# RetNet block and SwiGLU feed-forward on one core: the row norm of units 3 to 8 by block turns on VectorE and a 16-column product

## The chip, the cores and the metric

The kernel runs on one core of a Trainium2 chip. The metric is the device time of one execution in microseconds (us); the figure of a version is the median over its runs. The three runs of the kernel before took 1104.19, 1106.02 and 1107.22 us, so its median is 1106.02 us.

## The reference

Eight batches of eight heads, sequence 576, head size 64, go through a causal retention without softmax. The result is laid out as 4608 rows of 512 numbers and goes through an RMS norm and a SwiGLU feed-forward of inner width 1536. All of it is float32.

```python
scores = scale * np.matmul(q, k.transpose(0, 1, 3, 2))
gamma = 1.0 - 2.0 ** (-5.0 - np.arange(H, dtype=np.float32))
Dmat = np.where(rel >= 0, gamma[:, None, None] ** rel[None, :, :], 0.0)
x = np.matmul(scores * Dmat[None, :, :, :], v)            # -> (B*S, H*D)
rms = np.sqrt(np.mean(x * x, axis=-1, keepdims=True) + 1e-06)
xn = x / rms * rms_g
g = xn @ w_gate
out = (g * (1.0 / (1.0 + np.exp(-g))) * (xn @ w_val)) @ w_out
```

The part that matters here is `rms`: for each of the 4608 rows one sum of 512 squares, and the inverse root of it, with which the whole row is multiplied.

## The kernel before, in words

The 4608 rows are worked off in nine **units** of 512 rows, numbered 0 to 8. A unit's `x` lies turned in SBUF: the 512 features in four chunks of 128 partitions, the 512 rows along the free dimension (`x_of[u]`, 128 x 4 x 512). The sum over a row's features is therefore a sum over four chunks and 128 partitions.

Units 0 and 1 and the rounding of the weights are woven together by a written-out plan (`PLAN`, in `start`). From unit 2 on, one loop (lines 1283 to 1316) does for each unit u: six calls of `up(u, n)`, each 7 block products of a Strassen-like scheme (gate and value projections, into `h`); between them, up to four attention slots that make the `x` of later units; then `across(u)`, seven products of the output projection, again in blocks. Everything is issued in program order under a manual schedule, so the order on each engine is the order of the calls. `up` and `across` are generators that yield after each block product, and the loop puts the small steps of the next unit's norm behind chosen yields.

The norm of the next unit, u+1, stands as follows in this order:

- behind the first four products of `up(u, 5)`: `square` (line 458, ScalarE) squares chunk i, and `gather` (467, 473, VectorE) adds it to the running sum. After four chunks `t_of[u+1]` is one tile of 128 x 512 whose column sums are the sums of squares.
- behind the fifth product (i == 4): `root_1`. One matmul (504) multiplies the 128 x 512 tile with a 128 x 128 tile of ones, which leaves the column sums, the same in all 128 partitions, in a PSUM bank `ms`. Then an inverse square root by a guess from the bits and a polynomial step each, on full 128 x 512 tiles: ScalarE at 506, VectorE's `y` and `e` at 510 and 513, ScalarE's squares at 509 and 516, VectorE at 517.
- in `across(u)` behind the second yield after the first (i == 2): `root_2` (526, 529, VectorE, 128 x 512 tiles), which leaves the inverse root in an SBUF tile.
- i == 3 to 6: `scale_x` (548, VectorE), one chunk each: `x = x * rms_k * root`.
- i == 8: `sums_of_x` (563, VectorE): the block sums that the next unit's `up` multiplies.

All PSUM tiles come from one pool of eight banks. `up` takes four banks each call (`x`, `y`, `z`, `w`), `across` takes eight (`xo`, `xp` and so on, in the order of their products x, z, x, z, y, w, x), and `ms` one. `inner_sums` (766, 771, GpSimd) makes block sums that `across` multiplies; `second_operand` (775) and `last_operand` (779) are VectorE's share of the same. Units 0 and 1 have a norm of their own (`norm_1`, line 481: 16 products with one moving column each), and unit 2's `root_1` and `root_2` are called from the plan.

Of the kernel before, what the change touches and what calls it, by code (L numbers as in the profile page):

```python
# [10 lines left out]
F32 = mybir.dt.float32  # L11
U32 = mybir.dt.uint32
AF = mybir.ActivationFunctionType
ALU = mybir.AluOpType
P = 128
L = P // 2
SQ = 32
# [27 lines left out]
def kernel(  # L45
# [11 lines left out]
    nc = tc.nc  # L57
    B, H, S, D = q.shape
    NTOK, DM = out.shape
# [6 lines left out]
    U = 512  # L66
# [8 lines left out]
    K0, K1 = 2.38924456, 0.703952253  # L75
# [4 lines left out]
    const = ctx.enter_context(tc.tile_pool(name="const", bufs=1))  # L80
# [3 lines left out]
    tmp = ctx.enter_context(tc.tile_pool(name="tmp", bufs=4))  # L84
# [4 lines left out]
    def bank(name):  # L89
        return banks.tile([P, 512], F32, tag="b", name=name)  # L90
# [4 lines left out]
    def row(name):  # L95
        return tmp.tile([P, U], F32, tag="n", name=name, bufs=3)

    def cell(name, value):
        t = const.tile([P, 1], F32, name=name)
        nc.vector.memset(t, value)  # L100
        return t

    ones = const.tile([P, P], F32, name="ones")
    ident = const.tile([P, P], F32, name="ident")
# [3 lines left out]
    most = cell("most", 1151.0 + 7.5 / 16)  # L108
    top = cell("top", 255.0 * 2.0**23)
    guess = cell("guess", 0x5F1FFFF9 + 2.0**22 * np.log2(DM))  # L110
    causal = const.tile([P, L], F32, name="causal")
    gq = const.tile([P, NHP, L], F32, name="gq")
    gp = const.tile([P, NHP, 2], F32, name="gp")
# [36 lines left out]
    x_of, t_of = {}, {}  # L150
# [103 lines left out]
    def prepare(j):  # L254

        d = st[j]
        for odd in range(2):
            t = d["qraw"][:, odd::2]
            nc.scalar.activation(
                out=t, in_=t, func=AF.Copy, scale=gp[:, jobs[j][1], odd : odd + 1]  # L260
            )
        for nm in ("q", "k"):
            t = att.tile([P, S], F32, tag=nm + "T", name=f"{nm}T_{j}")
            nc.vector.transpose(out=t, in_=d.pop(nm + "raw").rearrange("p t a -> p (t a)"))
            d[nm + "T"] = t
        scale_v(j)
# [105 lines left out]
    def values(j):  # L372

        d = st[j]
        av = d["av"] = [bank(f"av_{j}_{i}") for i in range(2)]
        for c in range(NC):
            i, odd = divmod(c, 2)
            for e in range(2):
                mm = nc.tensor.matmul(  # L379
                    av[odd][column(j, odd, e), i * L : i * L + L],  # L380
                    lhsT=d["v"][side(odd), i, e] if c < NC - 1 else d["vt"][:, e],
                    rhs=d["ret"][side(odd), e, i],
                    start=(c < 2), stop=False, skip_group_check=True,
                )
        if j < FIRST:
            d["valued"] = nc.gpsimd.memset(tick, 0.0)
        else:
            d["valued"] = nc.scalar.copy(out=tick, in_=mhalf[:1])
        follow(d["valued"], mm)
# [41 lines left out]
    def slot(j, rest=True):  # L431

        if rest:
            values(j - 1)
        scores(j)
        states(j)
        weigh(j)
        if j < FIRST:
            sums(j)
        if rest:  # L440
            carried(j - 1)
        if j >= FIRST:
            sums(j)
# [5 lines left out]
    def fetch(j):  # L449
        if j < len(jobs):  # L450
            load_qk(j)
            load_kv(j)
# [3 lines left out]
    def square(u, c):  # L456
        t = row(f"sq_{u}_{c}")
        nc.scalar.activation(out=t, in_=x_of[u][:, c], func=AF.Square)
        return t
# [4 lines left out]
    def gather(u, c, sq):  # L464

        if c == NHP - 1 and u > 1:
            nc.vector.scalar_tensor_tensor(
                out=sq, in0=t_of[u], scalar=EPS * DM / P, in1=sq, op0=ALU.add, op1=ALU.add
            )
        elif u < 2 and c == NHP - 1:  # L470
            sq = (t_of[u], sq)
        elif c:
            nc.vector.tensor_tensor(out=sq, in0=t_of[u], in1=sq, op=ALU.add)
        t_of[u] = sq
# [24 lines left out]
    def root_1(u):  # L499


        y = t_of[u]
        s = bank(f"ms_{u}")
        nc.tensor.matmul(s, lhsT=ones, rhs=y, start=True, stop=True)
        e = row(f"e_{u}")
        nc.scalar.activation(
            out=y.bitcast(U32), in_=s.bitcast(U32), func=AF.Relu, bias=guess, scale=-0.5
        )
        nc.scalar.activation(out=e, in_=y, func=AF.Square)
        nc.vector.scalar_tensor_tensor(  # L510
            out=e, in0=e, scalar=-1.0 / DM, in1=s, op0=ALU.mult, op1=ALU.mult
        )
        nc.vector.scalar_tensor_tensor(
            out=y, in0=e, scalar=K0, in1=y, op0=ALU.add, op1=ALU.mult
        )
        nc.scalar.activation(out=e, in_=y, func=AF.Square)
        nc.vector.scalar_tensor_tensor(
            out=e, in0=e, scalar=K1 * K1 / DM, in1=s, op0=ALU.mult, op1=ALU.mult
        )
        t_of[u] = y, e  # L520

    def root_2(u):


        y, e = t_of[u]
        nc.vector.scalar_tensor_tensor(
            out=e, in0=e, scalar=-10.0 / 3.0, in1=e, op0=ALU.add, op1=ALU.mult
        )
        nc.vector.scalar_tensor_tensor(
            out=y, in0=e, scalar=5.0, in1=y, op0=ALU.add, op1=ALU.mult  # L530
        )
        t_of[u] = y

    def norm_2(u):
        scale_x(u, range(NHP))
# [223 lines left out]
    def inner_sums(u, n, part=None, eng=nc.gpsimd):  # L759

        x = operands_of(u)[order_of(u)[n]]
        x11, x12 = x[:, :NK, :P], x[:, :NK, P:]
        x21, x22 = x[:, NK:, :P], x[:, NK:, P:]
        i1, i3, i2, i4 = inner_of(u, n)
        if part != 1:
            eng.tensor_tensor(out=i1, in0=x12, in1=x11, op=ALU.subtract)  # L766
        c = slice(1, NK) if part == 1 else slice(0, 1) if part == 0 else slice(0, NK)
        for o, a, b, op in (
            (i3, x22, x12, ALU.subtract), (i2, i3, x11, ALU.add), (i4, x21, i2, ALU.subtract),
        ):  # L770
            eng.tensor_tensor(out=o[:, c], in0=a[:, c], in1=b[:, c], op=op)  # L771
# [244 lines left out]
    def store(u, b=None):  # L1016

        rows = out[u * U : u * U + U].rearrange("(C c p) (R r x) -> c r p C R x", C=2, c=2, R=2, r=2)
        v4 = vec.rearrange("p (C R) n d -> p C R n d", C=2)
        for n, (r, c) in CORNERS.items():  # L1020
            if b is None:
                for half in range(2):
                    nc.sync.dma_start(out=rows[c][r][:, half], in_=v4[:, half, :, n])
            else:
                nc.sync.dma_start(out=rows[c][r][:, b // 2, b % 2], in_=vec[:, b, n])
# [254 lines left out]
    with tc.manual_schedule():  # L1280
        start()
        for u in range(2, NU):
            j0 = NHP * (u + 1)
            more = u + 1 < B
            for n in range(2 * NG):
                for i, _ in enumerate(up(u, n)):
                    if n == 1 and i == 4:
                        store(u - 1)
                    if n == 2 * NG - 2 and i == 1:
                        inner_sums(u, 0, 0)  # L1290
                        inner_sums(u, 1, 0)
                    if more and i == 2 and 0 < n <= NHP:
                        if j0 + n < len(jobs):
                            prepare(j0 + n)
                            fetch(j0 + n + 1)
                    if u + 1 < NU and n == 2 * NG - 1:
                        if i < NHP:
                            gather(u + 1, i, square(u + 1, i))
                        elif i == NHP:
                            root_1(u + 1)  # L1300
                    if more and (n, i) == (NHP, 5) and j0 + NHP == len(jobs):
                        values(j0 + NHP - 1)
                if more and n <= NHP and (n or u == 2):
                    if j0 + n < len(jobs):
                        slot(j0 + n, rest=(n > 0))
                    else:
                        carried(j0 + n - 1)
            for i, _ in enumerate(across(u)):
                if u + 1 == NU:
                    continue  # L1310
                if i == 2:
                    root_2(u + 1)
                elif i in (3, 4, 5, 6):
                    scale_x(u + 1, (i - 3,))
                elif i == 8:
                    sums_of_x(u + 1)
# [27 lines left out]
```

## Time and profile before

| | us |
|---|---|
| runs | 1104.19, 1106.02, 1107.22 |
| span of the profiled execution | 1104.5 |
| PE busy | 1091.5 (99%) |
| VectorE busy | 751.7 (68%) |
| ScalarE busy | 339.7 (31%) |
| GpSimd busy | 458.0 (41%) |
| the product of line 504, 14 matmul instructions for 7 products | 7.2 |
| mean granted TensorE clock | 0.995 |

PE is TensorE's matmul, PEld its weight loads, DVE is VectorE, ACT ScalarE, POOL GpSimd. The span runs from the first instruction to the last of one profiled execution. One float32 product in the program is two weight loads and two matmul instructions in the profile, so the seven `ms` products are 14. Matmuls overlap in the pipeline, so the time that one takes from the stream is read as the distance of two starts and not as the duration of one.

### The profile page before, as it was taken

Reading aid. Unit: us, or ns where it says so; the run is one execution under the profiler, and the core shown is the slowest. Engines: PE = TensorE matmul, PEld = TensorE weight load, DVE = VectorE, ACT = ScalarE, POOL = GpSimd, SP = SyncE. Lnnn points to the kernel's source line nnn. Section 1 sums busy time; section 2 is a strip of 40 time slices with the busy share of each in tenths; the row PEclk is TensorE's granted clock in tenths of the full one; section 3 lists DMA queues with packets and bytes.
Section 4 is the critical chain, followed back from the end, with each engine's and each line's share of the span. In section 5 each row is a group of like instructions: output and inputs, shape, how many; then the busy total and the mean of one; then the engine's idle time right before and its main releaser. Section 6 shows DMA issues by size and latency. Waiting matters only on the chain.

```text
span 1104.5 us, 24454 instructions
## 1 busy us (share of the span) xinstructions
PE 1091.5 (99%) x10102; PEld 915.1 (83%) x10102; DVE 751.7 (68%) x1219; ACT 339.7 (31%) x757; POOL 458.0 (41%) x421
## 2 busy tenths in 40 slices
PE   8899999999999999999999999999999999999998
PEld 7654444479988899889988998889888998898898
DVE  3778568877866794678657775668565935594457
ACT  5855564331124412342034303330233111211110
POOL 0026325538430196027802581239321942393236
PEclk9899999999999999999999999999999999999999
DMA  8847777696978866787678865887475755585461
GB/s 211 197 139 259 280 244 217 208 343 185 289 277 227 216 251 226 185 238 235 253 215 199 285 259 149 245 246 284 143 203 198 273 193 176 183 293 158 152 247 43
DMA packets 253871, 243.60 MB, mean 221 GB/s; under 512 B 193216, under 2 KB 213824, under 8 KB 247616
## 3 DMA queue, kind: packets, MB, share of 16 engines
q1 hardware_dynamic: 252320, 241.64, 69.1%
q8 instruction: 79, 1.29, 0.5%
q10 hardware_dynamic: 1440, 0.40, 0.2%
q14 instruction: 32, 0.26, 0.1%
HBM read 211.92 MB, written 30.08 MB: 219 GB/s over the span
## 4 chain that ended last, share of the span: by engine, by line
PE 96%; DVE 1%; issue 1%; ACT 0%; POOL 0%; POOLq 0%; DVEq 0%; ACTq 0%
PE up L704 15%; PE x L644 14%; PE w L644 13%; PE z L644 13%; PE y L644 7%; PE xo L814 6%; PE xp L814 4%; PE zo L814 4%; PE zp L814 3%; PE wo L814 2%; PE yo L814 2%; PE av L379 2%; PE wp L814 2%; PE av L399 2%; PE s L292 2%; PE yp L814 2%
## 5 line engine op out<-in xcount | busy, mean ns | idle before, releaser
L704 PE MATMUL up<-x,ring 128*128 128x512 f32 x384 | 167.1, 595 | 0.0
L644 PE MATMUL x<-x,ring 128*128 128x256 f32 x672 | 161.1, 383 | 0.0
L644 PE MATMUL w<-sums,ring 128*128 128x256 f32 x672 | 158.9, 379 | 0.0
L644 PE MATMUL z<-x,ring 128*128 128x256 f32 x672 | 158.8, 379 | 0.0
L766 POOL TENSOR_TENSOR vi<-h 128x384 f32<-128x384 f32 x32 | 39.5, 1234 | 275.2 <-DVE h L663 266.3
L704 PEld LDWEIGHTS up<-x,ring 128*128 128x128 f32 x384 | 72.3, 190 | 89.3 <-issue 84.8
L644 PEld LDWEIGHTS z<-x,ring 128*128 128x128 f32 x672 | 127.8, 190 | 19.8 <-issue 2.9
L644 PEld LDWEIGHTS w<-sums,ring 128*128 128x128 f32 x672 | 127.7, 190 | 17.2
L644 PEld LDWEIGHTS x<-x,ring 128*128 128x128 f32 x672 | 125.5, 190 | 17.4 <-ACT m L670 0.2
L771 POOL TENSOR_TENSOR vi<-h 128x384 f32<-128x384 f32 (+2 forms) x46 | 46.4, 1009 | 149.5 <-DVE h L663 149.5
L1010 POOL TENSOR_TENSOR vi<-vi 128x512 f32<-128x512 f32 (+1 forms) x77 | 78.1, 1027 | 37.9 <-DVE vi L841 21.5
L644 PE MATMUL y<-sums,ring 128*128 128x256 f32 x336 | 79.4, 379 | 0.0
L670 ACT COPY m<-x 128x512 f32<-128x512 f32 x42 | 24.6, 586 | 173.4 <-PE x L644 173.4
L651 DVE TENSOR_TENSOR h<-u,w 128x512 f32<-128x512 f32 x42 | 28.9, 688 | 67.8 <-PE w L644 67.8
L651 DVE TENSOR_TENSOR u<-m,y 128x512 f32<-128x512 f32 x42 | 28.8, 687 | 63.4 <-PE y L644 62.7
L644 PEld LDWEIGHTS y<-sums,ring 128*128 128x128 f32 x336 | 63.9, 190 | 8.6
L665 ACT ACTIVATE h<-h 128x512 f32<-128x512 f32 x63 | 39.7, 630 | 84.1 <-DVE h L651 84.1
L1130 POOL TENSOR_TENSOR vi<-vi 128x512 f32<-128x512 f32 (+1 forms) x24 | 40.7, 1696 | 30.8 <-DVE vi L1119 17.3
L651 DVE TENSOR_TENSOR u<-u,z 128x512 f32<-128x512 f32 x42 | 28.9, 688 | 33.7 <-PE z L644 33.6
L1130 POOL TENSOR_TENSOR ring<-ring 128x512 f32<-128x512 f32 x24 | 30.4, 1272 | 49.3 <-DMA w_up_blocks<-ring 44.1
L771 POOL TENSOR_TENSOR vi<-vi,h 128x384 f32<-128x384 f32 (+2 forms) x46 | 47.6, 1034 | 3.6
L771 POOL TENSOR_TENSOR vi<-h,vi 128x384 f32<-128x384 f32 (+2 forms) x46 | 46.9, 1019 | 3.6
(314 smaller groups left out, 2086.5 us busy)
## 6 DMA issues: line engine op xcount, KB each, us to landing
ring<-w_out_blocks SPq DMA_DIRECT2D x59, 1344.0 KB, 6.4
ring<-w_up_blocks SPq DMA_DIRECT2D x42, 1792.0 KB, 7.7
w_out_blocks<-vi SPq DMA_DIRECT2D x21, 448.0 KB, 5.9
out_dram<-vi SPq DMA_DIRECT2D x64, 128.0 KB, 3.0
qraw<-in_q_dram SPq DMA_DIRECT2D x96, 72.0 KB, 5.1
kraw<-in_k_dram SPq DMA_DIRECT2D x96, 72.0 KB, 2.5
k<-in_k_dram SPq DMA_DIRECT2D x48, 128.0 KB, 2.9
v<-in_v_dram SPq DMA_DIRECT2D x48, 128.0 KB, 2.8
```

Source lines behind the costliest of these rows:

```text
L292: nc.tensor.matmul(s[e][side(odd), i * L : i * L + L], lhsT=d["kT"][side(e), c * L : c * L + L], rhs=d["qT"][side(e), c * L : c * L + L], ...
L379: mm = nc.tensor.matmul(av[odd][column(j, odd, e), i * L : i * L + L], lhsT=d["v"][side(odd), i, e] if c < NC - 1 else d["vt"][:, e], rhs= ...
L644: nc.tensor.matmul(ps[:, i * HU : i * HU + HU], lhsT=w[:, PLACE[blk], c, i * P : i * P + P], rhs=t_of[u][blk][:, c], start=(start and i == ...
L651: nc.vector.tensor_tensor(out=o, in0=a, in1=pairs_of(ps), op=ALU.add)
L665: nc.scalar.activation(out=o, in_=c, func=AF.Silu)
L670: nc.scalar.copy(out=s1, in_=pairs_of(x_))
L704: nc.tensor.matmul(ps, lhsT=w[:, PLACE[blk], c % 2, i * P : i * P + P], rhs=x_of[u][:, c], start=(c == 0), stop=(c == NHP - 1),)
L766: eng.tensor_tensor(out=i1, in0=x12, in1=x11, op=ALU.subtract)
L771: eng.tensor_tensor(out=o[:, c], in0=a[:, c], in1=b[:, c], op=op)
L814: nc.tensor.matmul(ps, lhsT=lhs[:, c], rhs=w[:, s, c], start=((nm, s // 4) not in first), stop=False, skip_group_check=True,)
L1010: eng.tensor_tensor(out=t[:, :, o], in0=t[:, :, x], in1=t[:, :, y], op=ALU.add)
L1130: nc.gpsimd.tensor_tensor(out=t[o], in0=t[x], in1=t[y], op=op)
```

## The change

For units 3 to 8 the steps change as follows; units 0, 1 and 2 stay as they are.

- `same_rows`, once, behind the second product of `up(2, 2)`: a constant 128 x 128 tile `alike`, one where two partitions have the same number modulo 32, made from the identity by one reduction and one copy on VectorE.
- `fold` takes the place of `root_1`'s product at i == 4: VectorE reduces the 128 x 512 tile with its 32 x 32 blocks turned, so that each of 16 blocks leaves a sum over its 32 partitions, and the result is 128 x 16.
- `meet` at i == 6, after the last product of `up(u, 5)`: one matmul of `alike` with that 128 x 16 tile. It adds what lies in the four groups of 32 partitions.
- `root` takes the place of `root_2` at i == 2 of `across(u)`: the guess and both steps on tiles of 128 x 16, eight instructions on VectorE and none on ScalarE, and then one block turn that reads each of the 16 columns 32 times and writes 128 x 512 into a PSUM bank `rows`.
- `scale_x` reads its factor from that PSUM bank and no longer from SBUF.

```diff
+    def same_rows():
+        t = tmp.tile([P, SQ], F32, tag="d", name="d", bufs=1)
+        nc.vector.tensor_reduce(
+            out=t, in_=ident.rearrange("p (a b) -> p b a", b=SQ), axis=mybir.AxisListType.X,
+            op=ALU.add,
+        )
+        nc.vector.tensor_copy(
+            out=alike.rearrange("p (a b) -> p a b", b=SQ),
+            in_=t.unsqueeze(1).to_broadcast([P, P // SQ, SQ]),
+        )
+    def fold(u):
+        t = column_of(f"fold_{u}")
+        nc.vector.tensor_reduce(
+            out=t, in_=t_of[u].rearrange("p (b j) -> p b j", j=SQ), axis=mybir.AxisListType.X,
+            op=ALU.add, apply_transpose=True,
+        )
+        t_of[u] = t
+    def meet(u):
+        t = t_of[u]
+        s = t_of[u] = bank(f"ms_{u}")[:, :NB]
+        nc.tensor.matmul(s, lhsT=alike, rhs=t, start=True, stop=True)
+    def root(u):
+        s = t_of[u]
+        y, e = column_of(f"y_{u}"), column_of(f"e_{u}")
+        def step(o, a, c, b, op0, op1=ALU.mult):
+            nc.vector.scalar_tensor_tensor(out=o, in0=a, scalar=c, in1=b, op0=op0, op1=op1)
+        nc.vector.tensor_scalar(
+            out=y.bitcast(U32), in0=s.bitcast(U32), scalar1=-0.5, scalar2=GUESS,
+            op0=ALU.mult, op1=ALU.add,
+        )
+        nc.vector.tensor_tensor(out=e, in0=y, in1=y, op=ALU.mult)
+        step(e, e, -1.0 / DM, s, ALU.mult)
+        step(y, e, K0, y, ALU.add)
+        nc.vector.tensor_tensor(out=e, in0=y, in1=y, op=ALU.mult)
+        step(e, e, K1 * K1 / DM, s, ALU.mult)
+        step(e, e, -10.0 / 3.0, e, ALU.add)
+        step(y, e, 5.0, y, ALU.add)
+        t_of[u] = bank(f"rows_{u}")
+        nc.vector.transpose(
+            out=t_of[u].rearrange("p (b j) -> p b j", j=SQ),
+            in_=y.unsqueeze(2).to_broadcast([P, NB, SQ]),
+        )
...
                         elif i == NHP:
-                            root_1(u + 1)
+                            fold(u + 1)
+                        elif i == 6:
+                            meet(u + 1)
+                    if (u, n, i) == (2, 2, 1):
+                        same_rows()
...
                 if i == 2:
-                    root_2(u + 1)
+                    root(u + 1)
```

More of the change, by code (lines that the diff above doesn't have):

```diff
@@ L110 @@
     guess = cell("guess", 0x5F1FFFF9 + 2.0**22 * np.log2(DM))
+    GUESS = float(0x5F1FFFF9 + 2.0**22 * np.log2(DM))
+    NB = U // SQ
+    alike = const.tile([P, P], F32, name="alike")
     causal = const.tile([P, L], F32, name="causal")
@@ L532, in root_2, with column_of @@
         t_of[u] = y
+    def column_of(name):
+        return tmp.tile([P, NB], F32, tag="c", name=name, bufs=3)
+    def same_rows():
[40 more added lines that the diff above has]
+        )
     def norm_2(u):
```

## The prediction

> **What bounds the kernel now.** I read the page's engine shares first, then the chain of work that ended last, then PE's waits, then the chain in order of time around one of the changed products.
>
> ```profile
> PE 1091.5 (99%) x10102; PEld 915.1 (83%) x10102; DVE 751.7 (68%) x1219; ACT 339.7 (31%) x757; POOL 458.0 (41%) x421
> ...
> PE 96%; DVE 1%; issue 1%; ACT 0%; POOL 0%; POOLq 0%; DVEq 0%; ACTq 0%
> ```
>
> PE is busy 99% of the span and is 96% of the chain. The list of PE's waits adds up to 8.7 us (2.3 + 1.7 + 1.4 + 1.2 + 0.5 + 0.4 + 0.4 + 0.3 + 0.3 + 0.2), and none of it stands before the norm's product, a product of `up` or a product of `across`. So time is won or lost only in PE's own stream: what PE no longer executes comes off the end, and what VectorE, ScalarE or GpSimd save is worth nothing unless PE waits for them. The chain in order of time around unit 3's product (start, us, what):
>
> ```profile
> 386.10 1.73 PE w L644 x8
> 387.83 0.86 PE ms L504 x2
> 388.69 1.73 PE z L644 x8
> 390.42 1.73 PE w L644 x8
> 392.14 1.34 PE xo L814 x12
> ```
>
> The reader sees a stream without a hole: the `ms` product takes 0.86 us between two block products of 1.73 us each.
>
> **The change on PE.** Six products with 512 moving columns go. Each costs 0.86 us, 5.1 us in all. Six with 16 moving columns come, at the end of `up(u, 5)`. The nearest row is the norm of units 0 and 1, with the same 128 x 128 weights and one moving column (start, us, instruction):
>
> ```profile
> 65.41 1.45 PE L704 MATMUL up<-x,ring 128*128 128x512 f32 x3
> 66.70 1.84 PE L481 MATMUL ms<-mean_w,sq 128*128 128x1 f32 x16
> 68.40 1.10 PE L704 MATMUL up<-x,ring 128*128 128x512 f32 x2
> ```
>
> Sixteen instructions fill 68.40 - 66.70 = 1.70 us, 0.106 us each, and a product is two: 0.21 us. The other such group, from 45.37 to 47.24, gives 0.117 and 0.23. Moving columns don't matter yet at this size: the output projection's 128-column instructions come every 0.112 us too (1.34 us for 12 above). So the row is that of a weight load and not of a matmul, and 16 columns lie between. I take 0.22. Bounds: the 64 x 64 products of line 399, 31 in 1.15 us, give 0.07 a pair from below; from above, add 0.085 to 0.22, because the first 512-column instruction after the group of 16 came 1.10 - 0.59 = 0.51 us before the next (one lasts 0.59 by its row) and the three before the group (1.45 - 0.59) / 2 = 0.43 apart, so a stream may need a moment to get its loads ahead again: 0.31. Saved per unit: 0.86 - 0.22 = 0.64 (0.55 to 0.79). **Six units: 3.8 us (3.3 to 4.7).**
>
> A rule stands beside this row. The Trainium skill, "TensorE: Matmul & The Clock Gate", section "Back-to-back issue gap", gives products of 1 to 64 columns an issue floor of about 25 ns; by that a pair would be 0.05 us and six units would win about 4.9 us (an estimate from that page). The same page, section "LDWEIGHTS (loading the stationary operand)", makes the load columns / 1.2 in ns, about 107 ns for 128 (its estimate), which gives 3.9 us. The row of 0.106 to 0.117 us sides with the second.
>
> **Does the moved product wait?** It now waits for `fold`, and behind it in PE's queue stands all of `across`. VectorE and PE around the place in before:
>
> ```profile
> 388.59 0.77 DVE L663 TENSOR_TENSOR h<-h,u 128x512 f32<-128x512 f32 x1
> 390.11 0.69 DVE L510 SCALAR_TENSOR_TENSOR e<-e,ms 128x512 f32<-128x512 f32 x1 [0.74 <-ACT e L509]
> 390.83 1.16 DVE L513 SCALAR_TENSOR_TENSOR sq<-e,sq 128x512 f32<-128x512 f32 x1
> 392.69 0.69 DVE L517 SCALAR_TENSOR_TENSOR e<-e,ms 128x512 f32<-128x512 f32 x1 [0.70 <-ACT e L516]
> ```
>
> `fold` stands behind L663 and before the `c12` and `c21` sums, so it starts at 388.59 + 0.77 = 389.36. PE reaches the product after two more blocks, at 387.67 + 2 x 1.73 = 391.13 (the timeline has the old product's start at 387.67; the chain counts from the end of what came before). That leaves 1.77 us. No row shows a reduction with turned blocks. Its nearest rows are VectorE's 128 x 512 instructions at 0.69 us and its block turns of 128 x 576, 0.736 to 0.771; the slowest 128 x 512 row, `scale_x` beside GpSimd, is 1.48. I take 0.7; even 1.48 is 0.3 early. Cost on the path: nothing; if the reduction took 2 us, 0.2 us a unit.
>
> **VectorE and ScalarE.** Per unit, five VectorE instructions go: 0.69 + 1.16 + 0.69 above, 1.21 and 1.37 for `root_2`, 5.1 us; with them go two waits for ScalarE, 1.4 us, and three ScalarE instructions. Ten come: `fold` 0.7; eight on 16 columns, bounded from above by the 128 x 64 rows (copy 0.215, scalar-tensor-tensor 0.281), at most 2.2 us; and the turn into PSUM, at 0.74 by
>
> ```profile
> L264 DVE STREAM_TRANSPOSE kT<-kraw x24: 731/736/739, 140.5 to 821.1; 128x576 f32<-128x576 f32 x24
> ```
>
> and at most 1.48: 3.6 to 4.4 us. `scale_x` took 5.58 us for four chunks beside GpSimd with its factor in SBUF; with its factor in PSUM the first units' rows are 0.743 each, 3.0 us. So VectorE gets shorter, and the next unit's `x` is ready earlier; `sums_of_x` ended at 416.28 and PE wants it at 424.81, a cover of 8.5 us. All this is hidden behind PE and I cost it at nothing. A rule speaks against the change here: the Trainium skill, "VectorE: DVE Perf Modes", section "Rules for kernel authors", says to keep the number of VectorE instructions small, since each pays its flush, and calls the reduction the slowest of its operations; ten for five would then be a loss. On the rows, 128 x 64 at 0.22 to 0.28 against 128 x 512 at 0.69 to 1.37, size still decides.
>
> `same_rows` adds about 0.5 us (two instructions of at most 0.28 by the 128 x 64 rows) once, before an instruction that idled 0.97 us for PE's `z`: hidden. The bank `rows` is the ninth in flight. In the changed program `across` gives its last pair, `wo` and `wp`, the banks of `ms` and `rows`; their first product is five blocks of 4.7 us into `across`, about 414.7, and `scale_x` ended at 408.2 in before. Hidden by 6 us.
>
> **The sum.** 1104.5 - 3.8 = 1100.7 us of span. The runs' median lies 1.5 us above that span, so the forecast is 1106.0 - 3.8 = **1102.2 us**, 0.34% less.
>
> **Rivals.**
>
> *A. The new wait eats the gain.* If `fold` takes over 1.77 us, or the product waits some other way, up to 0.64 us a unit comes back: 1102.2 to 1106. For it: a form that no row shows, right before its reader. Against: 1.48 is the slowest row near it. Chance 0.10.
>
> *B. Slower: GpSimd becomes late for `across`'s last product.* VectorE and GpSimd slow each other, and the tightest supply of PE is GpSimd's last block sum:
>
> ```profile
> 422.14 1.00 POOL L771 TENSOR_TENSOR vi<-t,vi 128x384 f32<-128x384 f32 x1
> ...
> 424.14 0.83 PE L814 MATMUL xo<-ring,vi 128*128 128x128 f32 x6
> ```
>
> Ready at 423.14, read at 424.14, so 1.0 us of cover, and PE now comes 0.64 earlier. If eight dependent instructions and the turn held VectorE, and through `last_operand` GpSimd, beyond that, PE would wait; from a delay of 1.0 us on, the kernel is slower than before (1.0 - 0.64 = 0.36 left as cover, then 0.64 of gain). A delay of 2 us costs 6 x 1.0, giving 1112. Against: GpSimd's own wait before 396.18 (0.63 us, for VectorE's L663) falls away, and instructions with two SBUF inputs are fewer. Chance 0.06.
>
> *C. The change does what it says and PE loses the time again,* waiting at the end of `across` for GpSimd, whose cover of 1.0 shrinks to 0.36, or for a weight block: within 0.3% of before, 1104 to 1106. Chance 0.06.
>
> **How the numbers follow.** My forecast has 0.78: with the bounds of the pair, 1101.3 to 1102.7, and some 1.3 us either way for the median of runs that spread over 3 us, 1100.0 to 1104.0. The range reaches into A and C: 1099.8 to 1105.0. A measurement of this kernel can tell about 0.3%, 3.3 us, from no change, so the boundary is 1102.7, close to the forecast: of the 0.78, 0.61 is faster by more and 0.17 within. A adds 0.01, 0.07 and 0.02; C 0.06 within; B 0.06 slower. Together 0.62, 0.30 and 0.08.
>
> **What would show it.** Right: the `ms` row at about 0.2 us in the chain, after the second `w` block, six times; no wait of PE at `ms`; the rest of the chain unchanged, 12 x 0.112 and 8 x 0.216 us; `scale_x` near 0.75 each; GpSimd's last block sum at least 0.4 us before its reader. Wrong: PE waiting for VectorE's `fold` (A), for GpSimd in `xo` (B, C), or an `xo` group that starts late after the new product with no wait, which would mean that the pair costs more than a load each.

## The result and the profile after

The changed kernel takes 1101.79 us (median of 8 runs) against 1106.66 for the kernel before, run beside it: a ratio of 0.9954, with a 95% interval of 0.9938 to 0.9969, which is a gain of 3.4 to 6.9 us. One of the eight runs was in a slow state, 1602.65 us at a mean granted clock of 0.654; the ratio leaves it out, and the median of the other seven is 1101.27 us. The forecast was 1102.2. The profiled execution has a span of 1098.4 us, 6.1 less than before, which is more than the sum foresaw; the first thing to settle is where the rest comes from.

The page of the kernel after, engine shares and chain:

```profile
PE 1085.5 (99%) x10102; PEld 912.2 (83%) x10102; DVE 727.2 (66%) x1251; ACT 328.2 (30%) x739; POOL 443.8 (40%) x421
...
PE 97%; DVE 1%; issue 1%; ACT 0%; POOL 0%; POOLq 0%; DVEq 0%; ACTq 0%
```

PE is still everything. VectorE lost 24.5 us of work (751.7 to 727.2), ScalarE 11.5 and GpSimd 14.2, and PE 6.0. PE's waits name neither `ms` nor a product of `across`. The chain in order of time around unit 3's product:

```profile
385.59 1.73 PE z L702 x8
387.32 1.73 PE w L702 x8
389.04 0.13 PE ms L565 x2
389.17 1.43 PE xo L872 x12
```

The pair takes 0.13 us, and the group after it 1.43 where twelve such instructions took 1.34 before: 0.09 more. Together 0.22, where before had 0.86. By the starts of single matmuls the pair and what it delays take 0.221 or 0.222 us in every one of the six units, against 0.857 to 0.859 for the old product. So six units give 6 x 0.636 = **3.8 us**.

The other 2.2 us lie ahead of the change. In before the old `ms` product of unit 3 starts at 387.67 us; in after the same point of the program, the end of the first `w` block, comes at 388.88 - 2 x 1.728 = 385.42. From this point to the end before takes 1104.51 - 387.67 = 716.84 us and after 1098.44 - 385.42 = 713.02, which is 3.82 less. Until there both kernels do the same work on PE. Nine traces (before, after and seven of the experiments below) have the same PE program up to unit 2's `ms` product, and it starts anywhere from 290.0 to 293.1 us, at 293.1 in before and 290.7 in after. A part of this is the granted clock, as the stretches view shows (stretch, its length, busy time of PE, PEld, DVE, ACT and POOL, granted clock, DMA share, GB/s); first before, then after:

```profile
10.00:20.00 10.00, 8.62 (x194) 7.39 (x191) 5.02 (x16) 4.24 (x12) 0.09 (x1) 0.83 0.85 217
...
40.00:50.00 10.00, 8.68 (x217) 7.71 (x211) 9.13 (x26) 6.70 (x19) 1.11 (x2) 0.96 0.89 240
50.00:60.00 10.00, 10.00 (x157) 6.45 (x155) 7.03 (x16) 4.45 (x10) 0.09 (x1) 0.70 0.67 178
```

```profile
30.00:40.00 10.00, 9.16 (x282) 7.96 (x279) 8.79 (x23) 9.32 (x25) 0.18 (x2) 0.83 0.78 179
```

Before ran 3.4 and 6.8 us at half clock in its first 60 us, after 3.4 us in one piece. These pieces change from run to run with the same program: 24 further runs of before had mean clocks from 0.993 to 1.000 and spans from 1101.1 to 1108.0 us. The lower the clock, the longer the span (correlation 0.66), but the clock is not the whole spread: two runs at 1.000 had spans of 1101.5 and 1104.0. The profiled pair happened to differ in it. The forecast of 3.8 us is a ratio of 0.9966, inside the measured interval.

On VectorE and GpSimd, the timeline of after (start, us, instruction, idle time before it and who ended it):

```profile
387.05 0.70 DVE L555 TRANSPOSE_TENSOR_REDUCE fold<-sq 128x16 f32<-128x512 f32 x1
...
395.11 0.16 DVE L575 TENSOR_SCALAR y<-ms 128x16 uint32<-128x16 uint32 x1
395.31 0.23 DVE L579 TENSOR_TENSOR e<-y 128x16 f32<-128x16 f32 x1
...
397.08 0.18 DVE L573 SCALAR_TENSOR_TENSOR y<-e,y 128x16 f32<-128x16 f32 x1
397.30 0.73 DVE L587 STREAM_TRANSPOSE rows<-y 128x512 f32<-128x512 f32 x1
398.06 2.72 DVE L606 SCALAR_TENSOR_TENSOR x<-x,rms_k,rows 128x512 f32<-128x512 f32 x4
405.45 2.16 DVE L837 TENSOR_TENSOR t<-h 128x1536 f32<-128x1536 f32 x1 [4.67 <-PE zp L872]
```

The reduction ends at 387.75 and PE comes for it at 388.88. The whole root takes 395.11 to 398.03, 2.9 us, and scaling 2.7 where it took 5.6. VectorE then stands 4.67 us, waiting for PE.

### The profile page after: what moved, and what is told of

Read it like the earlier page. It is cut to its first block, busy times and chain, and to the rows that moved or that the text cites. A ratio compares the mean times of both kernels' runs of the same rounds, so it can differ in the third digit from the quotient of the medians.

```text
span 1098.4 us, 24471 instructions
## 1 busy us (share of the span) xinstructions
PE 1085.5 (99%) x10102; PEld 912.2 (83%) x10102; DVE 727.2 (66%) x1251; ACT 328.2 (30%) x739; POOL 443.8 (40%) x421
## 3 DMA queue, kind: packets, MB, share of 16 engines
q8 instruction: 79, 1.29, 0.5%
## 4 chain that ended last, share of the span: by engine, by line
PE 97%; DVE 1%; issue 1%; ACT 0%; POOL 0%; POOLq 0%; DVEq 0%; ACTq 0%
PE up L762 15%; PE x L702 14%; PE w L702 13%; PE z L702 13%; PE y L702 7%; PE xo L872 6%; PE xp L872 4%; PE zo L872 4%; PE zp L872 3%; PE wo L872 2%; PE yo L872 2%; PE av L382 2%; PE av L402 2%; PE wp L872 2%; PE s L295 2%; PE yp L872 2%
## 5 line engine op out<-in xcount | busy, mean ns | idle before, releaser
L824 POOL TENSOR_TENSOR vi<-h 128x384 f32<-128x384 f32 x32 | 42.4, 1326 | 275.9 <-DVE h L721 266.4
L829 POOL TENSOR_TENSOR vi<-h 128x384 f32<-128x384 f32 (+2 forms) x46 | 43.9, 954 | 149.2 <-DVE h L721 149.2
L426 ACT COPY x<-av 128x192 f32<-128x192 f32 (+6 forms) x136 | 37.8, 278 | 30.0 <-PE av L402 28.5
L829 POOL TENSOR_TENSOR vi<-h,vi 128x384 f32<-128x384 f32 (+2 forms) x46 | 44.5, 968 | 3.6
```

Of the source, the lines that this page charges most:

```text
L426: nc.scalar.copy(out=o, in_=part)
```

## The experiments

The theory is that the gain is PE's stream and nothing else, and that the pair's price is that of two weight loads. Its rivals: relief of VectorE, ScalarE and GpSimd gives part of the gain (they lost 50 us of work together, and the profiled pair shows 2.2 us that the stream's product does not explain); the price is a floor for an instruction and a share for each column; the place of the product does not matter; VectorE's cover is small. Since the start varies by 3 us from trace to trace, the traces are also compared from the place of unit 3's old product to the end: 716.84 us in before, 713.02 in after.

### Other widths (e1_widths)

```diff
-        s = t_of[u] = bank(f"ms_{u}")[:, :NB]
-        nc.tensor.matmul(s, lhsT=alike, rhs=t, start=True, stop=True)
+        n = {3: 16, 4: 64, 5: 128, 6: 256, 7: 384, 8: 512}[u] // NB
+        s = bank(f"ms_{u}")[:, : n * NB].rearrange("p (b r) -> p b r", r=n)
+        nc.tensor.matmul(
+            s, lhsT=alike, rhs=t.unsqueeze(2).to_broadcast([P, NB, n]), start=True, stop=True
+        )
+        t_of[u] = s[:, :, 0]
```

> The new product gets another number of moving columns in each unit, by reading each of the 16 columns several times: 16, 64, 128, 256, 384 and 512 in units 3 to 8; the result is the same. Theory (the pair costs two weight loads of 0.11 us, and the columns hide behind them up to 128): the pair and the late load after it take 0.22, 0.22, 0.22 to 0.25 us from PE's stream at 16, 64 and 128 columns, then 0.43, 0.64 and 0.86. Rival (a floor for the instruction and then so much a column): 64 and 128 columns lie between 16 and 256 on a straight line, about 0.27 and 0.33. No wait of PE at any of them.

Measured from one start to the next, with the delay of the matmul after: 0.222, 0.221 and 0.222 us at 16, 64 and 128 columns, then 0.429, 0.642 and 0.856. The chain shows 128 and 256 columns:

```profile
621.71 0.22 PE ms L566 x2
621.93 1.34 PE xo L876 x12
```

```profile
737.16 0.43 PE ms L566 x2
737.59 1.34 PE xo L876 x12
```

At 128 columns the pair takes its 0.22 openly and the next group has its normal 1.34; at 16 it shows 0.13 and the group after pays 0.09. The sum is the same. So the step from 512 to 128 columns has the whole gain, and the last one, from 128 to 16, has none on PE. The line from 16 to 256 columns that the rival drew is not there.

### One, two, four and eight products; halves and quarters (e2_splits)

```diff
-        nc.tensor.matmul(s, lhsT=alike, rhs=t, start=True, stop=True)
+        w, n = {3: (P, 1), 4: (P, 2), 5: (P, 4), 6: (64, 1), 7: (32, 1), 8: (P, 8)}[u]
+        for _ in range(n):
+            for i in range(0, P, w):
+                nc.tensor.matmul(
+                    s[i : i + w], lhsT=alike[:, i : i + w], rhs=t, start=True, stop=True
+                )
```

> The new product is issued otherwise in each unit, with the same result: once in unit 3, twice in 4, four times in 5, in two products of 64 weight columns in 6, in four of 32 in 7, eight times in 8. Theory (cost goes by weight columns loaded): 0.22, 0.45, 0.89 and 1.79 us for one, two, four and eight; the two halves and the four quarters load the same 128 columns, so 0.22 plus some 0.1 for each change of the array's shape. Rival (cost goes by instruction): the halves 0.45 and the quarters 0.9.

One, two, four and eight: 0.222, 0.445, 0.891 and 1.784 us, 0.223 for each. The two halves take 0.327 and the four quarters 0.287, and the first of each came 0.093 later than after a full block: 0.42 and 0.38 with the two changes of the array's shape. Four quarters are eight instructions, and the rival had them at 0.9. The chain of the quarters:

```profile
853.14 0.18 PE ms L568 x8
853.33 1.54 PE xo L877 x12
```

Two whole loads cost 0.223 each time, and the same 128 columns in eight instructions cost less than half of the rival's price: it goes by weight columns loaded and not by instructions. Of the array's two changes of shape only the first, 0.093, is read by itself. If the load stays at 0.22, 0.11 is left for the second behind the halves and 0.07 behind the quarters.

### The product right behind its reduction (e3_at_once)

```diff
                             fold(u + 1)
-                        elif i == 6:
                             meet(u + 1)
```

> The product stands right behind the reduction that it reads, two block products earlier than in the change. Theory (the 1.7 us between them is the cover that keeps PE from waiting): PE waits for VectorE at the product in each unit, from its arrival at 385.4 to the end of the reduction at 387.8 by the times of the changed kernel, about 2.4 us; six units 14 us, the span near 1112. Rival (the place does not matter, PE runs ahead or the wait is hidden): no wait, the span within 3 us of 1098.

```profile
PE ms L565 <- DVE fold L555: 13.6, 6, 2.3
```

```profile
383.94 1.89 PE L702 MATMUL w<-sums,ring 128*128 128x256 f32 x8
388.12 0.37 PE L565 MATMUL ms<-fold,alike 128*128 128x16 f32 x2 [2.30 <-DVE fold L555]
388.34 1.97 PE L702 MATMUL z<-x,ring 128*128 128x256 f32 x8
```

The first line is from the list of PE's waits (us in total, times, longest), the others from PE's timeline in unit 3. PE waits 13.6 us for VectorE, 2.2 to 2.3 in each unit, as expected. But the span is 1120.3 and not near 1112: it is 21.9 us over the changed kernel, 21.7 of them behind the start. The stretches around the second and the fifth product show why (PE busy 6.92 us of 8 and 3.12 of 4; clock 0.79 and 1.00):

```profile
505.00:513.00 8.00, 6.92 (x32) 6.12 (x33) 3.70 (x6) 0.00 (x0) 5.39 (x8) 0.79 0.21 64
...
865.00:869.00 4.00, 3.12 (x16) 2.82 (x17) 1.59 (x4) 0.00 (x0) 3.84 (x6) 1.00 0.00 0
```

With three of the six pauses, in units 4, 5 and 6, the clock was halved, for 3.4, 6.8 and 3.4 us. The first two pieces begin 0.1 and 0.3 us before PE resumes, so PE runs 13.3 us at half clock and loses half of that, 6.6. By the starts of the matmuls a pause costs some 0.17 us more than the profile's wait, which counts from a modelled end, 14.6 in all, and the pair after a pause costs 0.30 instead of 0.22, 0.5 in all. That makes 21.7. So the place is what makes the change faster and not slower, and a wait of 2 us can cost more than itself.

### The whole cover of VectorE (e4_cover)

```diff
+        for _ in range({3: 1, 4: 7, 5: 12, 6: 17, 7: 23, 8: 28}[u]):
             nc.vector.transpose(
                 out=t_of[u].rearrange("p (b j) -> p b j", j=SQ),
```

> VectorE repeats the block turn into PSUM, so that everything behind it on VectorE comes later by about 0, 4.4, 8.0, 11.7, 16.1 and 19.7 us in units 3 to 8. Theory (VectorE's work is hidden by far: it waits 4.67 us for PE before the last operand and has 8 us more at the start of the next unit): no wait of PE in units 3 to 5, none or little in 6, about 4 us in 7 and 8 us in 8, so the span is 10 to 13 us longer. Rival (the cover is the 1.0 us that GpSimd's last block sum had before): PE waits in unit 4 already, by 3 us, then 7, 11, 15 and 19, about 55 us in all.

No wait in units 3 to 6, 3.5 us in 7 and 7.3 in 8, by the list of PE's waits and PE's timeline in unit 7:

```profile
PE wp L873 <- DVE x L607: 10.8, 2, 7.3
```

```profile
876.30 1.50 PE L873 MATMUL wo<-ring,h 128*128 128x128 f32 x12
881.33 1.65 PE L873 MATMUL wp<-ring,h 128*128 128x128 f32 x6 [3.53 <-DVE x L607]
```

A delay of 22 x 0.727 = 16.0 us left 3.5 and 19.6 left 7.3: the cover is 12.3 to 12.5 us. What came late was not GpSimd's block sum and not the next unit's `x` but the bank: `wp` gets that of `rows`, which is free only when `scale_x` has read it. The span is 1116.0, 17.6 over the changed kernel and so longer than expected. The start was 2.5 us longer (unit 3's product comes at 391.42). Of the other 15.0, the two pauses cost 11.2 by the starts of the matmuls. Both came with half clock again, 3.4 and 6.8 us, which began 0.4 and 2.4 us before PE resumed; PE ran 7.4 us at half clock and lost 3.7.

### PE's part alone (e5_wide_root)

```diff
-        s = t_of[u]
-        y, e = column_of(f"y_{u}"), column_of(f"e_{u}")
+        s = t_of[u].unsqueeze(2).to_broadcast([P, NB, SQ])
+        y, e = (row(f"{nm}_{u}").rearrange("p (b j) -> p b j", j=SQ) for nm in "ye")
...
-        nc.vector.tensor_tensor(out=e, in0=y, in1=y, op=ALU.mult)
+        nc.scalar.activation(out=e, in_=y, func=AF.Square)
...
-        t_of[u] = bank(f"rows_{u}")
-        nc.vector.transpose(
-            out=t_of[u].rearrange("p (b j) -> p b j", j=SQ),
-            in_=y.unsqueeze(2).to_broadcast([P, NB, SQ]),
-        )
+        t_of[u] = y.rearrange("p b j -> p (b j)")
```

> Only PE's part of the change is kept: the reduction and the 16-column product stand as in the change, but the root is the old one on 128 x 512, with its two squares and its guess on ScalarE, reading each of the 16 columns 32 times, and it leaves the factor in SBUF with no block turn. The rows then get the factor of another row of their block, so the output is not the reference's. Theory (all of the gain is PE's stream): as the changed kernel, a ratio near 0.996 to before, no wait of PE. Rival (relief of VectorE and ScalarE gives part of it): the ratio nearer to 1, 0.998 or more, since both engines have here a little more work than before.

A ratio of 0.996 (0.9943 to 0.9977), 1101.62 us. The changed kernel had 0.9954. No wait of PE. The factor in SBUF brings the old price of scaling back, and it costs next to nothing:

```profile
402.71 5.58 DVE L603 SCALAR_TENSOR_TENSOR x<-x,rms_k,y 128x512 f32<-128x512 f32 x4
408.21 2.55 DVE L834 TENSOR_TENSOR t<-h 128x1536 f32<-128x1536 f32 x1
```

Counted from the product, scaling ends 6 us later here than in the changed kernel (408.29 - 390.34 against 400.78 - 388.88), and VectorE has no idle time before the last operand. None of the relief is left: VectorE is busy for 755.0 us (751.7 before), ScalarE for 339.2 (339.7) and GpSimd for 459.9 (458.0). From the place of unit 3's old product to the end this kernel takes 713.24 us, 3.60 less than before and 0.22 more than the changed kernel.

### The relief without PE's part (e6_both)

```diff
+        nc.tensor.matmul(bank(f"old_{u}"), lhsT=ones, rhs=t_of[u], start=True, stop=True)
         t = column_of(f"fold_{u}")
```

> The changed kernel, and the old product of 512 columns is issued as well, at its old place, into a bank that nothing reads. So VectorE and ScalarE keep the relief and PE loses its saving. Theory: 6 x 0.22 = 1.3 us slower than before, a ratio of 1.001. Rival: still faster than before by the share that the relief gives, 0.998 or less.

A ratio of 1.0016 (1.0003 to 1.0029), where the two products' prices give 1.0012. The chain has both:

```profile
386.31 0.86 PE old L554 x2
387.17 1.73 PE z L703 x8
388.89 1.73 PE w L703 x8
390.62 0.13 PE ms L566 x2
```

With all of the relief and none of PE's saving the kernel is a little slower than before. From the old product's place to the end it takes 718.13 us, 1.29 more than before, and the six added pairs are 6 x 0.222 = 1.33. Together with the run above, this leaves at most some 0.2 us for the relief.

### A slow reduction (e9_slow_fold)

```diff
+        for _ in range({3: 1, 4: 2, 5: 3, 6: 4, 7: 5, 8: 7}[u]):
             nc.vector.tensor_reduce(
```

> VectorE makes the reduction 1, 2, 3, 4, 5 and 7 times in units 3 to 8, so its result comes later by 0, 0.7, 1.4, 2.0, 2.7 and 4.0 us (0.62 to 0.70 apart by the changed kernel's rows). It ended at 387.75 there and PE reached the product at 388.88, so the cover is 1.1 us. Theory (rival A of the prediction with its price): no wait in units 3 and 4, then about 0.3, 0.9, 1.6 and 2.9 us, and where PE stands still for more than some 2 us, a slice of 3.4 us at half clock may follow, as it did in four of six units when the product stood right behind the reduction. Rival (the pause alone counts): the span grows by the pauses and nothing else.

No wait in units 3 and 4, then 0.35, 1.00, 1.84 and 3.33 us; the list of PE's waits:

```profile
PE ms L566 <- DVE fold L556: 6.5, 4, 3.3
```

The repeated reductions came 0.74 us apart, more than expected, so the cover comes out at 1.1 to 1.2 us. The clock stayed whole with the first three waits and was halved for 6.8 us with the last, and only there, as the stretches around the products of units 7 and 8 show:

```profile
845.00:865.00 20.00, 18.16 (x135) 17.08 (x134) 18.41 (x28) 1.95 (x4) 16.41 (x18) 1.00 0.56 195
...
962.00:970.00 8.00, 7.47 (x40) 7.50 (x41) 7.30 (x12) 0.00 (x0) 5.28 (x6) 0.58 0.32 131
```

The span is 1108.4, 10.0 over the changed kernel, and 10.4 over it behind the start: 7.2 for the four waits by the starts of the matmuls, and 3.1 for the half clock, which began 0.6 us before PE resumed. The expectation above speaks of four of six units when the product stood right behind the reduction; it is three, the fourth slice lay in the first 60 us.

### The new norm in all units, and in unit 2 (e7_all_units, e8_unit_2)

```diff
-            "G": lambda j: gather(*squares.pop(0)), "N": norm_1, "D": diagonals, "X": norm_2,
+            "G": summed, "N": meet, "D": root, "X": norm_2,
...
-            "r": refill, "W": weights_to, "A": lambda u: next(outs[u], None), "R": root_1,
-            "Y": root_2, "M": sums_of_x, "o": store, "p": lambda _: later.pop()(),
+            "r": refill, "W": weights_to, "A": lambda u: next(outs[u], None), "R": meet,
+            "Y": root, "E": lambda _: same_rows(), "M": sums_of_x, "o": store, "p": lambda _: later.pop()(),
```

These are lines of the first. In the second, only `R` and `Y` of the plan, which make unit 2's norm, are replaced. In both, the reduction follows the fourth `gather`. In the first, the block turn also moves, in every unit, from the end of `root` to the start of `scale_x`.

> The new norm in all nine units: units 0 and 1 lose 16 matmul instructions at 0.112 us and a 512-column product at 0.86 and get the pair at 0.22, so 2.4 us each come off PE's stream, and unit 2 loses 0.64; GpSimd's power and ScalarE's diagonals go, VectorE gets about 3.5 us more in each of units 0 and 1. Theory: 5.5 us below the changed kernel, a ratio near 0.991 to before, if PE is the bound from 40 to 70 us too. Rival (VectorE, busy nine tenths from 30 to 60 us, becomes late there): PE waits for VectorE in that stretch and the ratio stays at 0.995 or above.

> The new norm in unit 2 as well, units 0 and 1 as before. Theory: the seventh pair costs 0.22 instead of 0.86 us in PE's stream, with no wait; 0.64 us cannot be told from the time of one execution, only from the trace. Rival (the reduction is late there, since VectorE still adds up the output of unit 1): PE waits at the product by some tenths of a us.

All units: a ratio of 0.9999 (0.9985 to 1.0012); the rival held. Unit 3 is reached at 390.52 us, 5.1 later than in the changed kernel. From 50 to 80 us, the kernel after the change first, then all units (PE, PEld, DVE, ACT, POOL):

```profile
50.00:60.00 10.00, 9.72 (x207) 6.16 (x205) 9.29 (x21) 5.76 (x14) 0.18 (x2) 1.00 0.60 118
60.00:80.00 20.00, 20.00 (x87) 10.19 (x82) 15.19 (x27) 13.40 (x26) 6.03 (x5) 1.00 0.46 172
```

```profile
50.00:60.00 10.00, 7.14 (x144) 4.62 (x144) 9.58 (x27) 2.90 (x5) 0.09 (x1) 0.83 0.75 184
60.00:80.00 20.00, 15.19 (x96) 6.89 (x95) 18.29 (x38) 8.97 (x15) 5.17 (x5) 0.91 0.17 54
```

The longest of the new waits, from the list of PE's waits in all units:

```profile
PE up L763 <- DVE sums L1161: 4.3, 1, 4.3
```

VectorE goes from 24.5 to 27.9 us of 30, PE falls from 29.7 to 22.3. There VectorE rounds the weights that PE waits for, and the same ten instructions that are free in unit 3 stand ahead of it. VectorE's timeline in unit 1:

```profile
69.24 1.25 DVE L577 TENSOR_TENSOR e<-y 128x16 f32<-128x16 f32 x1
...
73.24 0.17 DVE L571 SCALAR_TENSOR_TENSOR y<-e,y 128x16 f32<-128x16 f32 x1
...
74.65 0.69 DVE L1161 SCALAR_TENSOR_TENSOR sums<-sums,man 128x512 f32<-128x512 uint32 x1
```

With GpSimd at work beside them the eight small ones take 4.4 us here (69.04 to 73.41), against 1.6 in unit 0, where GpSimd has next to nothing to do. Not all of the loss is shown to be VectorE's: of PE's waits from 50 to 80 us, 8.9 in all, 4.9 are for VectorE and 3.7 have no cause in the profile ("issue"), and two pieces of half clock, 3.4 us each, lie there as well.

Unit 2 alone: the pair costs 0.224 us with no wait, so another 0.64 us comes off the stream. One execution at 1103.53 us cannot show 0.06%.

## Why the prediction was right, point by point

- **PE alone decides.** Right: PE's part alone gave 0.996, the relief alone 1.0016, and the traces from unit 3 on leave at most some 0.2 us for the relief.
- **The pair at 0.22 us, six units 3.8 us.** Right to the hundredth (3.82 in the traces), and for the reason given: the load, not the columns. What the prediction did not have is how it is paid. The second matmul starts 0.028 us after the first, the next one 0.112 later, and the `xo` matmul after that takes 0.192 to its successor and not 0.112: 0.08 us of debt. The row of 16 instructions shows the same. Its 1.70 us lack the debt, which is the 0.51 in place of 0.43 behind it; with it the 16 take 1.78, 0.223 a pair. So the 0.22 that the prediction took had the debt in it already, and the upper bound counted it a second time.
- **The time, 1102.2 us.** That it lies within 1 us of the measured median is partly luck. The measured ratio is 5.1 us of gain and the sum 3.8, and the runs spread over 5 us; they cannot tell the two apart. That the gain is 3.8 rests on the traces.
- **The rule of 25 ns for products of up to 64 columns** (the Trainium skill, "TensorE: Matmul & The Clock Gate", section "Back-to-back issue gap") would have given 4.9 us. A start 0.028 us after the one before does occur here, but once in a group, between its first two instructions; the others come 0.112 apart, and the 0.08 is paid behind the group. The section "LDWEIGHTS (loading the stationary operand)" of the same page has the price that eight products in a row confirm to 5%: they measured 0.223 for two loads, and its formula gives 0.213 (an estimate from that page).
- **The wait for `fold`.** Right in size: 0.70 us, as taken, and a cover that one more reduction did not use up and two more overran by 0.35. The point from which rival A decides, 1.77 us, came out as 0.70 + 1.13 = 1.83. Its price was too low: with three of six pauses of 2.2 to 2.3 us and with one of 3.3, half clock came on top.
- **VectorE hidden.** Right. Eight small instructions took 2.15 us against a bound of 2.2, the turn 0.73 against 0.74, scaling 0.743 each as in the first units. The Trainium skill, "VectorE: DVE Perf Modes", section "Rules for kernel authors", says to keep the number of instructions small and calls the reduction the slowest operation. Neither decided here: ten instructions took 0.70 + 2.15 + 0.73 = 3.6 us in place of five with 5.1, and the reduction took no longer than an elementwise instruction of its size, 0.70 against 0.69.
- **The bank.** The prediction named it and gave it 6 us, counted from where `scale_x` ended in before. It was 12.3 to 12.5, since `scale_x` now ends at 400.8; but when VectorE was delayed, it was the first thing to come late, ahead of GpSimd's last block sum and of the next unit's `x`, which the prediction had with covers of 1.0 and 8.5 us.
- **Rivals B and C.** Wrong in direction: they had GpSimd's last block sum at a cover that shrinks from 1.0 to 0.36 us. It grew:

```profile
416.21 1.74 POOL L829 TENSOR_TENSOR vi<-t,vi 128x384 f32<-128x384 f32 x1
...
421.26 0.83 PE L872 MATMUL xo<-ring,vi 128*128 128x128 f32 x6
```

Ready at 417.95, read at 421.26: 3.3 us. Counted from unit 3's old product, `last_operand` ends only 0.8 us earlier. The rest is GpSimd's own: while scaling reads its factor from PSUM, and while VectorE then stands, its block sums take 1.00 us. They took 1.32 to 1.44 beside scaling from SBUF. One of them in before, and the same in after:

```profile
403.50 1.32 POOL L771 TENSOR_TENSOR vi<-vi,t 128x384 f32<-128x384 f32 x1
```

```profile
399.85 1.00 POOL L829 TENSOR_TENSOR vi<-vi,t 128x384 f32<-128x384 f32 x1
```

With the factor back in SBUF (e5_wide_root) they take 1.32 to 1.46 again. So the prediction looked at what VectorE might hold up and not at what GpSimd gains when VectorE does less beside it.

- **What the profiled pair hid.** By its 6.1 us the forecast of 3.8 would look much too small. The 2.2 us above it lie ahead of the first changed product.

## What to carry to other kernels

A matmul that stands in a full stream costs its columns or its weight load, whichever is longer, so shrinking the moving side pays until both are equal (here, in float32 with 128 weight columns, at 128 moving columns) and no further. What moves to another engine is free only in the stretch where that engine waits: the same ten VectorE instructions cost nothing in units 3 to 8, and in units 0 and 1, where they were to save some 5 us, the kernel with them fell back to the time of before. When the difference of two profiles is larger than the sum of the step's own times, look whether it arose before the first changed instruction, and compare the two from there to the end.

## What the runs showed of the hardware

- Half clock comes in pieces of 3.4 or 6.8 us. In the middle of the run it came with pauses of PE: with none of 0.35, 1.00 and 1.84 us, with three of six of 2.2 to 2.3, and with each of 3.3, 3.5 and 7.3. The length alone does not decide: two pauses of 2.21 us and one of 2.30 had it, three of 2.30 did not. In every trace all pieces start a whole number of 3.413 us apart, as on a fixed grid. Behind the first 100 us a piece started or went on after each interval of this grid in which PE's pauses made up 1.93 us or more, and none started after an interval with 1.91 or less; the two values are too close to call this a threshold. In the first 60 us less was enough, and what sets the length of a piece is not shown.
- VectorE's 16-column instructions take 0.16 to 0.18 us. Those that read SBUF twice took 0.22 to 1.25 us in places with GpSimd at work, while those that read PSUM and SBUF stayed at 0.17; the block reductions and block turns stayed at 0.70 to 0.73 throughout.
